# Four operands of a linear-attention kernel turned by block loads and 32x32 VectorE transposes

## The chip, the cores and the metric

The kernel runs on one core of one Trainium2 chip. The metric is the device time in microseconds, as the median of several runs. The core has five engines that each work through a queue of their own in order: TensorE (PE in the profile, its weight loads PEld), VectorE (DVE), ScalarE (ACT), GpSimd (POOL) and SyncE (SP, which here only issues DMAs). DMAs can be issued from SP's queue and from ScalarE's.

## What is computed

First a recurrence with a 40x40 state for each of 4 x 8 (batch, head) pairs over 768 tokens, then a mixture of four experts over 3072 tokens of width 320:

```
for t in range(S):
    y[:, :, t] = einsum('bhd,bhde->bhe', rt, state)
    Sa = einsum('bhde,bhe->bhd', state, at)
    state = state * wt[:, :, None, :] - einsum('bhd,bhe->bhde', Sa, bt) + einsum('bhd,bhe->bhde', vt, kt)
x = y with (batch, token) as rows and (head, channel) as 320 columns
p = domain_probs / (domain_probs.sum(-1) + 1e-9)
out = sum over e of p[:, e] * (relu(x @ w1[e]) @ w2[e])        # w1[e]: 320 x 1024
```

All of it is float32. Inputs r, k, v, w, a, b are stored as (batch, head, token, channel), so that a row of 40 channels, 160 bytes, is contiguous.

## The kernel before

**Units.** Tokens are taken in chunks of 64. A unit is one chunk of two batches, all eight heads: 24 units, in order of chunk. Its 128 partitions are 2 x 64 tokens ("token-major"), or, after a turn, 2 x 64 channels of a pair of heads of which 40 count ("channel-major"). Within a unit the recurrence is rewritten as matrix products between 64 tokens, with decays accumulated along the chunk, and a triangular solve in 32x32 blocks.

**Loads.** `load` brings each operand token-major, one DMA for each batch; V and R take three each, since their heads 4 to 7 are stored with neighbours swapped. All go through SP, 20 issues a unit (L188). Loads for unit u + 3 are issued in the loop's round u.

**`within(q)`** is the part of a unit that needs no state. It is a generator: each `yield` ends a piece, and the loop says which piece comes where. Its first piece turns W on TensorE (`turn`, L295: four transposes of 128x128 against the identity into one PSUM bank), copies it from PSUM on ScalarE one token to the right (L346) and takes the running product along tokens with a VectorE scan (L347): G, channel-major. `gl` is the product over the whole chunk. The second piece turns G back (pg) and forms gp = pg * W and a_tok = pg * A on VectorE, the reciprocal of gp (L365), and turns R and V. Then n_tok = -B / gp and k_tok = K / gp (L392, L395). Then A, N and K are turned and copied (`turned`, L369), and the score matrices are formed by `quadrants` (L327: 32 small matmuls, in 64x64 quarters of the array): `pc` from R and V, `pf` and `pe` from A, N, K; `pev` follows. `causal` is a masked copy on VectorE (L334).

**`substitute`** is the triangular solve: blocks of F are turned by VectorE into M (L445, L448), and a chain of some 66 operations follows on GpSimd, or on VectorE for units 0 and 1. `merge` turns the result Z back by two 32x32 transposes (Qc L495, QTc L497) and completes it with TensorE products pY, pQ; ScalarE copies it into QT (L527). **`step`** carries the state: prn (AT and state), psat, pxr, then pdy and the state's update. Its output Y goes to xT, channel-major, by small DMAs (L639), or by TensorE (L627) for the first units.

**The mixture** is cut into pieces that stand in a list `todo`: an `up` piece (24 matmuls, L654 and L662, then two ScalarE activations L667) or a `down` piece (L769, then adds on VectorE L680 and, after every second one, sums of hidden activations L763). w1 streams in pieces through SP (L238). `mix(n)` emits the next n pieces; `gap(0)` to `gap(3)` do this four times in each round of the loop, two pieces each in most rounds. So PE has mixture pieces between the recurrence's parts.

**Order.** The framework schedules what it is given; `keep_in_program_order` pins an instruction against the other pinned ones. PSUM has five banks for the recurrence ("big") and three for the mixture ("mm").

Of the kernel before, what the change touches and what calls it, by code (L numbers as in the profile page):

```python
# [15 lines left out]
def kernel(  # L16
# [12 lines left out]
):  # L29

# [98 lines left out]
    def kept(name, shape, n, value=0.0, eng=nc.gpsimd, lo=0):  # L129
# [15 lines left out]
    nat = {  # L145
        x: kept(f"nat{x}", of_64, n, float(x == "W"), nc.vector, D) for x, n in (("W", 2), ("R", 2), ("V", 2))
    }
    a_tok = kept("a_tok", of_64, 1, lo=D)
# [25 lines left out]
    def load(q, names):  # L174
        for x in names:
            if x in nat:
                t = nat[x]()
            else:
                t = sb.tile([P, H, D], FP32, name=f"nat{x}")
            q.n[x] = t  # L180
            for i, bb in enumerate(q.b):
                to, src = t[i * L:(i + 1) * L, :, 0:D], srcs[x][bb, :, q.c * L:(q.c + 1) * L, :]
                parts = ((slice(0, H), slice(0, H)),)
                if x in "VR":

                    parts = ((slice(0, 4), slice(0, 4)), (slice(5, H, 2), slice(4, H, 2)), (slice(4, H, 2), slice(5, H, 2)))
                for o, h in parts:
                    nc.sync.dma_start(out=to[:, o, :], in_=src[h].rearrange("h t e -> t h e"))  # L188
# [3 lines left out]
    for u, names in ((0, "W"), (1, "W"), (0, "ABKVR")):  # L192
        load(units[u], names)
# [111 lines left out]

    def head(j, s):
        return 2 * j + s

    def d_half(j, s):
        return s ^ (j // 2)  # L310

    def d_head(j, s):
        return 2 * j + d_half(j, s)

    BY_TOKENS = [(j, s, i) for j in range(NJ) for s, i in QUADS]
    BY_PAIRS = [(j + 2 * x, s, i) for i in range(2) for j in range(2) for s, x in QUADS]
# [16 lines left out]
    def causal(to, data):  # L333
        return nc.vector.copy_predicated(  # L334
            out=to, mask=mask_up[:, None, :].to_broadcast([P, data.shape[1], L]), data=data,
        )

    def within(q):

        n = q.n  # L340
        pw = by(turn("pw", tok(n["W"]))[:], L)
        q.G = G = sb.tile([P, 2 * NJ, L], FP32, name="G", tag="G", bufs=3)
        ins = nc.vector.memset(G[:, :, 0:1], 0.0)
        if q.u == 1:
            tc.keep_in_program_order(ins)
        nc.scalar.copy(out=G[:, :, 1:L], in_=pw[:, :, 0:L - 1])  # L346
        ins = nc.vector.tensor_tensor_scan(  # L347
            out=G[:].rearrange("p c i -> p (c i)"), data0=G[:].rearrange("p c i -> p (c i)"),
            data1=first[:].rearrange("p c i -> p (c i)"), initial=0.0, op0=ALU.mult, op1=ALU.add,
        )  # L350
        if q.u == 1:
            tc.keep_in_program_order(ins)
        q.gl = sb.tile([P, 2 * NJ, 1], FP32, name="gl", tag="gl", bufs=4)
        nc.scalar.copy(out=q.gl[:], in_=pw[:, :, L - 1:L])
        nc.vector.tensor_tensor(out=q.gl[:], in0=q.gl[:], in1=G[:, :, L - 1:L], op=ALU.mult)
        yield

        pg = by(turn("pg", tok(G), q.u == 2)[:], 64)[:, :, 0:D]
        gp = sb.tile([P, H, D], FP32, name="gp")
        ins = nc.vector.tensor_tensor(out=gp[:], in0=pg, in1=n["W"][:, :, 0:D], op=ALU.mult)  # L360
        if q.u == 1:
            tc.keep_in_program_order(ins)
        A = a_tok()
        nc.vector.tensor_tensor(out=A[:, :, 0:D], in0=pg, in1=n["A"][:], op=ALU.mult)
        nc.vector.reciprocal(out=gp[:], in_=gp[:])  # L365

        def turned(name, x, keep=False):
            t = sb.tile([P, NJ, P], FP32, name=name, tag=name if keep else "turned", bufs=2 if keep else 3)
            nc.scalar.copy(out=t[:].rearrange("p j t -> p (j t)"), in_=turn("p" + name, tok(x), q.u == 1)[:])  # L369
            return t  # L370

        def turn_rv():
            q.RT = turned("RT", n["R"], True)
            return turned("VT", n["V"])

        def causal_scores(VT):
            pc = quadrants(banks("pc"), 0, BY_TOKENS, L, lambda j, s, i: (
                d_half(j, s), i, j, of_pairs(VT, d_half(j, s), j, i), of_pairs(q.RT, d_half(j, s), j, i),
            ))
            for s in range(2):  # L380
                ins = causal(of_slot(q.VC[:], s)[:, :, D:D + L], pc[s])
                if q.start:
                    tc.keep_in_program_order(ins)

        if q.u == 1:
            yield
        if q.u > 0:
            VT = turn_rv()
            yield
# [5 lines left out]
        nc.vector.tensor_tensor(out=q.K[:, :, 0:D], in0=n["K"][:], in1=gp[:], op=ALU.mult)  # L395
        q.VC = VCs()
        if q.u > 0:
            nc.scalar.copy(out=q.VC[:, :, 0:D], in_=n["V"][:, :, 0:D])
        yield

        q.AT = turned("AT", A, True)
# [4 lines left out]
        if q.u > 0:  # L406
            causal_scores(VT)
# [4 lines left out]
            s, i ^ s, j, of_pairs(q.AT, s, j, i), of_pairs(NT, s, j, i),  # L412
        ))
        pe = quadrants(p, NJ * L, BY_TOKENS, L, lambda j, s, i: (
            s, i, j, of_pairs(KT, s, j, i), of_pairs(q.AT, s, j, i),
# [9 lines left out]
        if q.u == 0:  # L425
            tc.keep_in_program_order(nc.scalar.copy(out=q.VC[:, :, 0:D], in_=n["V"][:, :, 0:D]))
        q.EV = EVs()
        pev = quadrants(banks("pev"), 0, BY_TOKENS, D, lambda j, s, i: (
            i, i ^ s, j, ET[half(i), head(j, s), :], q.VC[half(i), d_head(j, s), 0:D],
# [571 lines left out]
```

## Time and profile before

| | us |
|---|---|
| median of 3 runs | 1162.93 (1161.68 to 1165.82) |
| profiled execution | 1161.04 |
| its span, first to last instruction | 1159.3 |
| PE busy | 1134.2 |
| DVE busy | 693.6 |
| ACT busy | 385.4 |
| POOL busy | 472.5 |
| DMA moved | 107.45 MB in 218853 packets |

The profile is one execution. Its page has the engines' busy times, the span in 40 slices, and groups of instructions by line, with busy time, the mean duration in ns, and the idle time ahead of them with what ended it. The chain of waits is followed back from the last instruction. Matmuls overlap in PE's pipeline, so their distance counts and not their duration.

### The profile page before, as it was taken

The numbers are of one execution on the slowest core, as the hardware profiler recorded it, in microseconds if no ns is written. First come the engines' busy times: TensorE is split into PE (matmuls) and PEld (weight loads), VectorE is DVE, ScalarE is ACT, GpSimd is POOL, SyncE is SP. The second block draws the span as 40 slices with busy tenths as digits, with TensorE's granted clock in tenths as the row PEclk, the third lists the DMA queues.
The fourth block names the chain that finished last, engine by engine and source line by source line (L and its number), as shares of the span: only waits on it lengthen the run. The fifth ranks groups of instructions, "written<-read, shape, count | busy, mean of one in ns | idle before, by whom it ended". The sixth has DMA issues, their size and how long they took to land.

```text
span 1159.3 us, 38763 instructions
## 1 busy us (share of the span) xinstructions
PE 1134.2 (98%) x16400; PEld 1014.2 (87%) x16400; DVE 693.6 (60%) x1466; ACT 385.4 (33%) x961; POOL 472.5 (41%) x1218
## 2 busy tenths in 40 slices
PE   7999999999999999999999999999999999999998
PEld 6887787798988999898989899998889898988887
DVE  7754556775665575666746655756567566543333
ACT  3332444334233333333342333333333423311110
POOL 4006555572462552643724625526336246240000
PEclk8899999999999999999999999999999999999999
DMA  4695433323333333243333333342333341221320
GB/s 68 196 278 109 106 76 85 88 67 92 94 93 94 86 89 98 65 112 71 93 93 85 100 96 78 91 96 73 101 75 93 91 105 49 76 88 52 104 91 12
DMA packets 218853, 107.45 MB, mean 93 GB/s; under 512 B 163720, under 2 KB 192056, under 8 KB 218680
## 3 DMA queue, kind: packets, MB, share of 16 engines
q1 hardware_dynamic: 218600, 104.93, 35.1%
q8 instruction: 130, 2.13, 0.7%
q14 instruction: 43, 0.35, 0.1%
q10 hardware_dynamic: 80, 0.04, 0.0%
HBM read 97.04 MB, written 3.93 MB: 87 GB/s over the span
## 4 chain that ended last, share of the span: by engine, by line
PE 92%; DMA 2%; ACT 2%; SPq 2%; issue 1%; DVE 1%; ACTq 0%; DVEq 0%
PE ph L662 30%; PE p L769 29%; PE ph L654 9%; PE pdy L327 3%; PE po L703 2%; PE psat L327 2%; PE pfe L327 2%; PE pxr L327 2%; SPq L188 2%; PE prn L327 2%; PE pc L327 1%; PE pQ L522 1%; PE pY L510 1%; PE pev L327 1%; DMA w<-in_moe_w_dram 1%; PE pg L295 1%
## 5 line engine op out<-in xcount | busy, mean ns | idle before, releaser
L662 PE MATMUL ph<-xT,w1p 128*128 128x256 f32 (+1 forms) x1520 | 343.6, 379 | 0.1
L471 POOL TENSOR_TENSOR Z<-M,Z 128x62 f32<-128x62 f32 (+7 forms) x352 | 164.8, 468 | 404.4 <-DVE M L464 378.5
L662 PEld LDWEIGHTS ph<-xT,w1p 128*128 128x128 f32 x1520 | 274.6, 191 | 62.3 <-issue 26.0
L484 POOL TENSOR_TENSOR Z<-Z 128x31 f32<-128x31 f32 (+7 forms) x704 | 247.3, 351 | 55.2
L763 DVE TENSOR_TENSOR a<-hs 128x512 f32<-128x512 f32 x220 | 153.5, 715 | 186.4 <-ACT hs L667 186.4
L667 ACT ACTIVATE hs<-ph 128x512 f32<-128x512 f32 (+1 forms) x208 | 117.2, 564 | 304.7 <-PE ph L662 304.2
L769 PE MATMUL p<-sums,a 128*128 128x160 f32 x1056 | 164.8, 299 | 0.0
L680 DVE SCALAR_TENSOR_TENSOR osb<-p,gate,osb 128x320 f32<-128x320 f32 (+1 forms) x243 | 108.4, 484 | 93.7 <-PE p L769 88.6
L769 PEld LDWEIGHTS p<-sums,a 128*128 128x128 f32 x1056 | 152.9, 190 | 2.2
L654 PE MATMUL ph<-xT,w1p 64*128 64x256 f32 (+1 forms) x760 | 109.6, 395 | 1.5 <-PE psat L327 1.0
L769 PE MATMUL p<-w,hs 128*128 128x160 f32 x704 | 102.9, 299 | 0.0
L769 PE MATMUL p<-w,a 128*128 128x160 f32 x704 | 102.8, 299 | 0.0
L769 PEld LDWEIGHTS p<-w,hs 128*128 128x128 f32 x704 | 100.2, 190 | 2.2
L769 PEld LDWEIGHTS p<-w,a 128*128 128x128 f32 x704 | 98.0, 190 | 0.0
L654 PEld LDWEIGHTS ph<-xT,w1p 64*128 64x128 f32 x760 | 67.2, 186 | 13.7 <-issue 3.3
L503 POOL COPY QT<-QTc 32x256 f32<-32x256 f32 x96 | 38.8, 404 | 97.1 <-DVE QTc L497 87.3
L448 DVE STREAM_TRANSPOSE M<-blocks 128x1024 f32<-128x1024 f32 x24 | 47.0, 1957 | 33.1 <-ACT blocks L445 32.4
L365 DVE RECIPROCAL gp<-gp 128x320 f32<-128x320 f32 x24 | 51.3, 2137 | 0.0
L527 ACT COPY QT<-pQ 32x256 f32<-32x256 f32 x48 | 17.4, 362 | 83.3 <-PE pQ L522 82.8
L369 ACT COPY RT<-pRT 128x512 f32<-128x512 f32 x24 | 14.1, 586 | 93.1 <-PE pRT L295 93.0
L595 ACT COPY RS<-pxr 64x256 f32<-64x256 f32 x88 | 32.3, 367 | 34.9 <-issue 25.9
L327 PE MATMUL pdy<-VC,k_tok 64*64 64x104 f32 (+1 forms) x768 | 38.8, 261 | 0.0
(143 smaller groups left out, 1423.5 us busy)
## 6 DMA issues: line engine op xcount, KB each, us to landing
w1p<-in_moe_w_dram SPq DMA_DIRECT2D x95, 512.0 KB
w1p<-in_moe_w_dram SPq DMA_DIRECT2D x190, 64.0 KB
w<-in_moe_w_dram SPq DMA_DIRECT2D x4, 1280.0 KB
sums<-in_moe_w_dram SPq DMA_DIRECT2D x9, 512.0 KB
natW<-in_w_dram SPq DMA_DIRECT2D x48, 80.0 KB
natA<-in_a_dram SPq DMA_DIRECT2D x48, 80.0 KB
natB<-in_b_dram SPq DMA_DIRECT2D x48, 80.0 KB
natK<-in_k_dram SPq DMA_DIRECT2D x48, 80.0 KB
```

The costliest lines, as they stand in the source:

```text
L327: nc.tensor.matmul(out=p[row][half(col), lo + at * out_cols:lo + (at + 1) * out_cols], lhsT=lhsT, rhs=rhs, start=(n == 0), stop=(n == len( ...
L365: nc.vector.reciprocal(out=gp[:], in_=gp[:])
L448: ins = nc.vector.transpose(out=M[:], in_=cols)
L471: ins = eng.tensor_tensor(out=Z[:, 1:3, 0:n, j + 1:Q], in0=M[:, j:j + 2, None, j + 1:Q].to_broadcast([P, 2, n, m]), in1=Z[:, here, 0:n, j: ...
L484: eng.tensor_tensor(out=z[:, 0], in0=z[:, 0], in1=z[:, x], op=ALU.add)
L503: ins = nc.gpsimd.tensor_copy(out=q.QT[quarter(i), :, quarter(i % 2)], in_=QTc[quarter(i)])
L654: nc.tensor.matmul(out=ph[i][:, f, :], lhsT=w1.last[i * DT:(i + 1) * DT, f, :], rhs=xT[i * DT:(i + 1) * DT, 2, :], start=(f == 0), stop=False,
L662: nc.tensor.matmul(out=ph[i][:, f, :], lhsT=w1.main[:, g, at * P:(at + 1) * P], rhs=xT[:, g, :], start=False, stop=(g == 1 and f == HF // ...
L667: nc.scalar.activation(out=h[:, i * HF // 2:(i + 1) * HF // 2, 0:n], in_=ph[i][:], func=ACTF.Relu,)
L680: nc.vector.scalar_tensor_tensor(out=to, in0=p, scalar=sc, in1=to, op0=ALU.mult, op1=ALU.add)
L763: nc.vector.tensor_tensor(out=t[:], in0=x, in1=y, op=op)
L769: nc.tensor.matmul(out=p[:, n * HD:(n + 1) * HD], lhsT=a[:, f, :], rhs=b[:, f, :], start=(f == 0), stop=(f == HF - 1),)
```

## The change

W, A, R and V are no longer turned on TensorE. `load_raw` brings each of them in blocks. The 16 heads of a unit are taken in pairs, and partitions are pairs of neighbouring tokens. A block has 32 token pairs on 32 partitions and, for each head, 72 or 48 contiguous values: channels 0 to 31 of both tokens (with what lies between), or channels 32 to 39. Four such blocks fill 128 partitions: W and A take 4 DMAs each, R and V 8 each, since every second head of theirs goes to the other half ("d swapped by odd pairs"). Each has one buffer. `turn_raw` then transposes 32x32 squares on VectorE, 128x512 in one instruction, with the two tokens of a pair written side by side; W takes two of 128x256. The scan's input, VT, RT and AT come from that directly, channel-major. A's product with its decay is taken channel-major (AT * G, 128x512), after the turn, where it was taken token-major from PSUM (pg * A, 128x320) before. `gl` is a small VectorE copy. W, B, K and V are also loaded token-major, one DMA for each batch; A and R are not.

V's and R's heads go to the halves by `s ^ (j % 2)` where it was `s ^ (j // 2)`; the token-major V is no longer swapped, and the orders of the quadrant products and the masked copies follow. The turns of V and R stand in the third piece of `within`, after k_tok, and A's too.

In the loop SP issues W's and A's blocks (8) and the natural loads (8) of unit u + 3. V's and R's 16 blocks go into a list `later`, from which ScalarE issues three after each mixture piece (six where a gap has one piece), pinned; what is left goes ahead of the next unit's third piece. At the start, ScalarE issues unit 0's A and V blocks and SP the rest, and 20 warm-up matmuls stand where there were 6 and 4.

```diff
@@ -142,10 +146,8 @@
     srcs = {"W": w, "A": a, "B": b, "K": k, "V": v, "R": r}
     of_64 = [P, H, 64]
-    nat = {
-        x: kept(f"nat{x}", of_64, n, float(x == "W"), nc.vector, D) for x, n in (("W", 2), ("R", 2), ("V", 2))
-    }
-    a_tok = kept("a_tok", of_64, 1, lo=D)
+    raw = {x: kept(f"raw{x}", [P, 2 * NJ, 2 * D], 1, 0.0, nc.vector, D + D - Q) for x in "WARV"}
     k_tok, n_tok = (kept(x, of_64, 2, lo=D) for x in ("k_tok", "n_tok"))
     both = [P, H, D + L]
@@ -173,24 +175,51 @@
     def load(q, names):
         for x in names:
-            if x in nat:
-                t = nat[x]()
-            else:
-                t = sb.tile([P, H, D], FP32, name=f"nat{x}")
-            q.n[x] = t
+            q.n[x] = t = sb.tile([P, H, D], FP32, name=f"nat{x}", tag=f"nat{x}", bufs=2 if x in "WV" else 1)
             for i, bb in enumerate(q.b):
-                to, src = t[i * L:(i + 1) * L, :, 0:D], srcs[x][bb, :, q.c * L:(q.c + 1) * L, :]
-                parts = ((slice(0, H), slice(0, H)),)
-                if x in "VR":
-                    parts = ((slice(0, 4), slice(0, 4)), (slice(5, H, 2), slice(4, H, 2)), (slice(4, H, 2), slice(5, H, 2)))
-                for o, h in parts:
-                    nc.sync.dma_start(out=to[:, o, :], in_=src[h].rearrange("h t e -> t h e"))
+                nc.sync.dma_start(
+                    out=t[i * L:(i + 1) * L], in_=srcs[x][bb, :, q.c * L:(q.c + 1) * L, :].rearrange("h t e -> t h e"),
+                )
+    def load_raw(q, names):
+        moves = []
+        for x in names:
+            q.n["raw" + x] = t = raw[x]()
+            heads = srcs[x].rearrange("b h t e -> (b h) t e")[q.b[0] * H:(q.b[1] + 1) * H, q.c * L:(q.c + 1) * L, :]
+            heads = heads.rearrange("n (x two) e -> x n (two e)", two=2)
+            for r in range(2):
+                if x in "RV":
+                    sets = ((slice(0, 8, 2), slice(r, 16, 4)), (slice(1, 8, 2), slice(3 - r, 16, 4)))
+                else:
+                    sets = ((slice(0, 8), slice(r, 16, 2)),)
+                for n, hs in sets:
+                    for y, w_ in enumerate((D + Q, 2 * D - Q)):
+                        o = slice(64 * r + Q * y, 64 * r + Q * y + Q)
+                        moves.append(lambda eng, out=t[o, n, 0:w_], in_=heads[:, hs, Q * y:Q * y + w_]: eng.dma_start(out=out, in_=in_))
+        return moves
+    def go(moves, eng=None):
+        for move in moves:
+            move(eng or nc.sync)
+    def turn_raw(out, t):
+        return nc.vector.transpose(
+            out=out.rearrange("p n (x two) -> p n two x", two=2),
+            in_=t.rearrange("p n (two e) -> p n two e", two=2)[:, :, :, 0:Q],
+        )
     for u in range(3):
         begin(u)
-    for u, names in ((0, "W"), (1, "W"), (0, "ABKVR")):
-        load(units[u], names)
+    go(load_raw(units[0], "W"))
+    load(units[0], "WBK")
+    go(load_raw(units[0], "A"), nc.scalar)
+    load(units[0], "V")
+    go(load_raw(units[0], "V"), nc.scalar)
+    go(load_raw(units[0], "R"))
@@ -303,17 +332,21 @@
     def of_pairs(x, hf, j, i):
         return x[half(hf), j, part(i)]
+    def of_slots(x, hf, j, i, n=64):
+        return x[64 * hf:64 * hf + n, 4 * i + j, :]
     def head(j, s):
         return 2 * j + s
     def d_half(j, s):
-        return s ^ (j // 2)
-    def d_head(j, s):
-        return 2 * j + d_half(j, s)
+        return s ^ (j % 2)
+    def of_d_half(x, r):
+        return x.rearrange("p (jj four) e -> p jj four e", four=4)[:, :, slice(1, 3) if r else slice(0, 4, 3), :]
...
     def within(q):
         n = q.n
-        pw = by(turn("pw", tok(n["W"]))[:], L)
-        q.G = G = sb.tile([P, 2 * NJ, L], FP32, name="G", tag="G", bufs=3)
-        ins = nc.vector.memset(G[:, :, 0:1], 0.0)
-        if q.u == 1:
-            tc.keep_in_program_order(ins)
-        nc.scalar.copy(out=G[:, :, 1:L], in_=pw[:, :, 0:L - 1])
-        ins = nc.vector.tensor_tensor_scan(
-            out=G[:].rearrange("p c i -> p (c i)"), data0=G[:].rearrange("p c i -> p (c i)"),
+        def pin(ins, also=False):
+            if q.u == 1 or also:
+                tc.keep_in_program_order(ins)
+        G = sb.tile([P, 2 * NJ * L + 1], FP32, name="G", tag="G", bufs=3)
+        q.G = Gv = G[:, 0:2 * NJ * L].rearrange("p (c t) -> p c t", t=L)
+        ahead = G[:, 1:2 * NJ * L + 1].rearrange("p (j i t) -> p i j t", i=2, t=L)
+        for i in range(2):
+            pin(turn_raw(ahead[:, i], n["rawW"][:, NJ * i:NJ * i + NJ, :]))
+        q.gl = sb.tile([P, 2 * NJ, 1], FP32, name="gl", tag="gl", bufs=4)
+        pin(nc.vector.tensor_copy(out=q.gl[:, :, 0], in_=G[:, L::L]))
+        pin(nc.vector.memset(Gv[:, :, 0:1], 0.0))
+        pin(nc.vector.tensor_tensor_scan(
+            out=G[:, 0:2 * NJ * L], data0=G[:, 0:2 * NJ * L],
             data1=first[:].rearrange("p c i -> p (c i)"), initial=0.0, op0=ALU.mult, op1=ALU.add,
-        )
-        if q.u == 1:
-            tc.keep_in_program_order(ins)
-        q.gl = sb.tile([P, 2 * NJ, 1], FP32, name="gl", tag="gl", bufs=4)
-        nc.scalar.copy(out=q.gl[:], in_=pw[:, :, L - 1:L])
-        nc.vector.tensor_tensor(out=q.gl[:], in0=q.gl[:], in1=G[:, :, L - 1:L], op=ALU.mult)
-        yield
-        pg = by(turn("pg", tok(G), q.u == 2)[:], 64)[:, :, 0:D]
+        ))
+        nc.vector.tensor_tensor(out=q.gl[:], in0=q.gl[:], in1=Gv[:, :, L - 1:L], op=ALU.mult)
+        yield
+        pg = by(turn("pg", tok(Gv), q.u == 2)[:], 64)[:, :, 0:D]
         gp = sb.tile([P, H, D], FP32, name="gp")
-        ins = nc.vector.tensor_tensor(out=gp[:], in0=pg, in1=n["W"][:, :, 0:D], op=ALU.mult)
-        if q.u == 1:
-            tc.keep_in_program_order(ins)
-        A = a_tok()
-        nc.vector.tensor_tensor(out=A[:, :, 0:D], in0=pg, in1=n["A"][:], op=ALU.mult)
+        pin(nc.vector.tensor_tensor(out=gp[:], in0=pg, in1=n["W"][:], op=ALU.mult))
         nc.vector.reciprocal(out=gp[:], in_=gp[:])
-        def turned(name, x, keep=False):
-            t = sb.tile([P, NJ, P], FP32, name=name, tag=name if keep else "turned", bufs=2 if keep else 3)
+        yield
+        def turned(name, x):
+            t = sb.tile([P, NJ, P], FP32, name=name, tag="turned", bufs=3)
             nc.scalar.copy(out=t[:].rearrange("p j t -> p (j t)"), in_=turn("p" + name, tok(x), q.u == 1)[:])
             return t
-        def turn_rv():
-            q.RT = turned("RT", n["R"], True)
-            return turned("VT", n["V"])
-        def causal_scores(VT):
+        def causal_scores():
             pc = quadrants(banks("pc"), 0, BY_TOKENS, L, lambda j, s, i: (
-                d_half(j, s), i, j, of_pairs(VT, d_half(j, s), j, i), of_pairs(q.RT, d_half(j, s), j, i),
+                d_half(j, s), i, j, of_slots(VT, d_half(j, s), j, i, D), of_slots(q.RT, d_half(j, s), j, i, D),
             ))
-            for s in range(2):
-                ins = causal(of_slot(q.VC[:], s)[:, :, D:D + L], pc[s])
-                if q.start:
-                    tc.keep_in_program_order(ins)
-        if q.u == 1:
-            yield
-        if q.u > 0:
-            VT = turn_rv()
-            yield
+            for r in range(2):
+                pin(causal(of_d_half(q.VC[:, :, D:D + L], r), pc[r]), q.start)
         q.K, q.N = k_tok(), n_tok()
         nc.vector.scalar_tensor_tensor(
             out=q.N[:, :, 0:D], in0=n["B"][:], scalar=-1.0, in1=gp[:], op0=ALU.mult, op1=ALU.mult,
         )
         nc.vector.tensor_tensor(out=q.K[:, :, 0:D], in0=n["K"][:], in1=gp[:], op=ALU.mult)
+        q.AT = sb.tile([P, 2 * NJ, L], FP32, name="AT", tag="AT", bufs=2)
+        turn_raw(q.AT[:], n["rawA"][:])
+        at_ij = q.AT[:].rearrange("p (i j) t -> p i j t", i=2)
+        nc.vector.tensor_tensor(out=at_ij, in0=at_ij, in1=Gv.rearrange("p (j i) t -> p i j t", i=2), op=ALU.mult)
         q.VC = VCs()
         if q.u > 0:
-            nc.scalar.copy(out=q.VC[:, :, 0:D], in_=n["V"][:, :, 0:D])
-        yield
-        q.AT = turned("AT", A, True)
+            nc.scalar.copy(out=q.VC[:, :, 0:D], in_=n["V"][:])
+        VT = sb.tile([P, 2 * NJ, L], FP32, name="VT", tag="turned", bufs=3)
+        q.RT = sb.tile([P, 2 * NJ, L], FP32, name="RT", tag="RT", bufs=2)
+        turn_raw(VT[:], n["rawV"][:])
+        turn_raw(q.RT[:], n["rawR"][:])
+        yield
         NT = turned("NT", q.N)
         KT = turned("KT", q.K)
         yield
         if q.u > 0:
-            causal_scores(VT)
+            causal_scores()
             yield
...
@@ -571,29 +602,26 @@
...
         yield
         p = banks("pxr")
         px = quadrants(p, 0, BY_TOKENS, L, lambda j, s, i: (
-            d_half(j, s), i, j, SaT[half(d_half(j, s)), j, i ^ s, :], of_pairs(q.RT, d_half(j, s), j, i),
+            d_half(j, s), i, j, SaT[half(d_half(j, s)), j, i ^ s, :], of_slots(q.RT, d_half(j, s), j, i),
         ))
         if not q.start:
             prs = quadrants(p, NJ * L, BY_PAIRS, L, lambda j, s, i: (
-                d_half(j, s), s, 2 * (j % 2) + i, SN[half(d_half(j, s)), s, 2 * i + j % 2, :],
-                of_pairs(q.RT, d_half(j, s), j, i),
+                d_half(j, s), s, 2 * (j // 2) + i, SN[half(d_half(j, s)), s, 2 * i + j // 2, :],
+                of_slots(q.RT, d_half(j, s), j, i),
             ))
         for x in range(2):
...
@@ -825,12 +853,19 @@
             before = [lambda e=e: down_1(e), lambda e=e, second=second: second(e)]
         last[:] = before
-    todo, last = [], []
+    todo, last, later = [], [], []
+    def begin_later(n):
+        for move in later[:n]:
+            tc.keep_in_program_order(move(nc.scalar))
+        del later[:n]
     def mix(n):
         for piece in todo[:n]:
             piece()
+            begin_later(3 if n > 1 else 6)
         del todo[:n]
     def run(gen, n=99):
@@ -856,11 +891,13 @@
             tc.keep_in_program_order(ins)
     ws = [within(units[u]) for u in range(3)]
-    keep_warm(6)
+    keep_warm(20)
     run(ws[0], 1)
-    keep_warm(4)
+    go(load_raw(units[1], "W"))
     run(ws[0], 1)
-    load(units[1], "ABKVR")
+    load(units[1], "WBKV")
+    run(ws[0], 1)
+    go(load_raw(units[1], "AVR"))
     load_probs()
     run(ws[1], 1)
     run(ws[0], 2)
@@ -870,15 +907,16 @@
     m, s = merge(units[0]), begin_step(0)
     run(m, 1)
     run(ws[0])
-    load(units[2], "WVR")
+    go(load_raw(units[2], "W"))
+    load(units[2], "WBKV")
     for e in range(2):
         load_piece()
         load_piece()
         load_w2(e)
     run(ws[1], 1)
     keep_warm(36)
-    run(ws[1], 2)
-    load(units[2], "ABK")
+    run(ws[1], 1)
+    go(load_raw(units[2], "AVR"))
     load_piece()
     run(m)
     run(s, 4)
@@ -900,7 +938,8 @@
     run(ws[2], 2)
     run(s, 2)
     run(ws[2], 1)
-    load(begin(3), srcs)
+    load(begin(3), "WBKV")
+    go(load_raw(units[3], "WAVR"))
     substitute(units[2], nc.gpsimd)
     mix(1)
     w_next = ws[2]
@@ -938,13 +977,16 @@
             mixture_of_unit(q)
         elif q.bp:
             mixture_of_chunk(units[u - 1:u + 1], chunks_x[q.c])
+        begin_later(len(later))
         run(w, 1)
         if not early:
             run(m, 1)
         gap(1)
         if u + 3 < NU:
-            load(begin(u + 3), srcs)
+            go(load_raw(begin(u + 3), "WA"))
+            load(units[u + 3], "WBKV")
+            later.extend(load_raw(units[u + 3], "VR"))
         run(w, 2)
         if not early:
             run(s_next, 1)
```

## Prediction

> **What bounds the kernel now.** I read the page first, its engine table and its 40 slices.
>
> ```profile
> span 1159.3 us, 38763 instructions
> PE 1134.2 (98%) x16400; PEld 1014.2 (87%) x16400; DVE 693.6 (60%) x1466; ACT 385.4 (33%) x961; POOL 472.5 (41%) x1218
> PEclk8899999999999999999999999999999999999999
> DMA  4695433323333333243333333342333341221320
> ```
>
> TensorE is busy for 98% of the span and its granted clock is full after the second slice; DMA is heavy only in slices two and three. A busy PE may hide waits, so I next read the chain of waits, in order of time, around one unit in the middle:
>
> ```profile
> 601.34 0.44 PE pw L295 x4
> 601.77 0.60 PE pev L327 x32
> ...
> 612.39 0.44 PE pg L295 x4
> 612.83 0.44 PE pRT L295 x4
> 613.27 0.44 PE pVT L295 x4
> 613.70 1.74 PE pdy L327 x61
> ...
> 623.42 0.44 PE pAT L295 x4
> 623.85 0.44 PE pNT L295 x4
> 624.29 0.44 PE pKT L295 x4
> 624.73 0.62 PE pc L327 x32
> ```
>
> Nothing but PE is on it, and pw returns 45.36 us later: that is one unit. Each group of four transposes takes 0.44 us of PE's queue (not the 0.27 us that one matmul is shown to last, since they overlap). The windows view over exactly one unit says how much room the others have:
>
> ```profile
> 600.00:645.36 45.36, 45.36 (x686) 41.18 (x686) 28.19 (x59) 16.02 (x40) 20.25 (x51) 1.00 0.32 86
> ```
>
> The columns are PE, PEld, DVE, ACT, POOL, then clock, DMA share and GB/s: PE 45.36 of 45.36, VectorE 28.19, ScalarE 16.02.
>
> **The change, part by part.** *TensorE.* pw, pRT, pVT and pAT go; pg, pNT and pKT stay. 4 x 0.44 = 1.76 us a unit, all on the path. Units 2 to 23 have theirs where PE carries the path: 22 x 1.76 = 38.7 us. Units 0 and 1 belong to the start, below. The quadrant products keep their number and sizes; only their order changes (nothing).
>
> *VectorE.* It gains three 128x512 turns (A, V, R), two of 128x256 (W), one 128x512 product and a small copy, and loses a_tok. The trace has these rows (busy us, mean ns):
>
> ```profile
> L495 DVE STREAM_TRANSPOSE Qc<-Z 128x256 f32<-128x256 f32 x24 | 15.1, 628 | 36.6 <-POOL Z L484 36.6
> L497 DVE STREAM_TRANSPOSE QTc<-Qc 128x256 f32<-128x256 f32 x24 | 10.7, 445 | 0.6
> L461 DVE TENSOR_TENSOR Z<-M 128x512 f32<-128x512 f32 x24 | 16.6, 691 | 0.7
> ```
>
> A 128x512 turn lies between 0.69 us (any 512-column operation) and 1.26 (twice Qc, whose writes are scattered). I take twice QTc, 0.89, for it reads whole runs of 32 as the new turns do; their writes step by only two elements. W's halves are 0.45 each. Sum: 3 x 0.89 + 2 x 0.45 + 0.70 + 0.17 (gl, as L355) - 0.48 (a_tok) = 4.0 us; VectorE goes from 28.2 of 45.4 to 32.2 of 43.6, 74%. Average room is not enough, so I follow the tight stretch. At 610.26 VectorE begins the adds of a down piece and runs without a gap to the end of k_tok at 619.99, now 0.40 sooner without a_tok: 619.6. Then come A's turn, its product, V's and R's turn, 3 x 0.89 + 0.70 = 3.4: 623.0. PE wants them at pc, which moves from 624.73 up by three turns (1.32) to 623.4: 0.4 us to spare. Qc and QTc (1.08) follow, done at 624.05 for pY at 626.28 - 1.32 = 624.96. So I put the cost at nothing, but the cover is thin: at 0.69 a turn it is 1.0 us, at 1.26 pc is 0.7 us late. W's turns fall in a 3.5 us hole of VectorE before the sums of hs at 608.7, and cost nothing; were that hole shut, the 1.2 us would meet PE's next down piece.
> The Trainium skill, page "VectorE: DVE Perf Modes", section "Rules for kernel authors", speaks against this: for a whole 128x128 transpose it prefers TensorE where PSUM will do. By it each tensor pays 0.45 us more (0.89 against 0.44), a loss where VectorE were the bound; the unit above shows that PE is.
>
> *ScalarE and the loads.* ScalarE loses the copies of pw (0.58 + 0.17), RT, VT and AT (0.59 each): 2.5 us. It gains 16 DMA issues a unit, V's and R's blocks, six per gap. The issues of natV on SP last 0.595/0.606/1.514 us (min/median/max). Sixteen at 0.62 are 9.9 us, so ScalarE goes to 23.4 of 43.6. What counts is who is queued behind them. Six stand after the activation that ends at 632.26; the next there is QT's copy, which waits for pQ (ends 636.59) and which psat needs at 637.68:
>
> ```profile
> 631.66 0.60 ACT L667 ACTIVATE hs<-ph 128x512 f32<-128x512 f32 x1 [1.07 <-PE ph L662]
> 636.64 0.75 ACT L527 COPY QT<-pQ 32x256 f32<-32x256 f32 x2 [4.38 <-PE pQ L522]
> ```
>
> 6 x 0.62 = 3.7 us in a hole of 4.4: nothing, so long as an issue stays under 0.72 us. The one issue of before that ScalarE makes (the last store) took 0.56 us while SP was issuing too.
> SP has 16 issues a unit (8 raw W and A, 8 natural) where it had 20: 2.5 us less. Its raw A must wait for VectorE's turn of the unit before, as each raw tile has one buffer; behind it stand B, K, V, the xT moves and w1p. SP runs ahead of PE there: it waits 263 us in all (L238, for PE ph) until a w1p buffer is free. Packets: a unit had 6 x 1024 of 160 bytes; now 4 x 1024 of these and 4 x 1024 of 288 or 192. 2048 more at the queue's mean (35.1% x 16 x 1159.3 / 218600 = 30 ns) are 3.8 us of the sixteen engines: share 0.32 to 0.42, hidden. V's and R's last four issues follow the activation that ends at 608.7, so they end by 611.2 and land by 613.2 (1.97 us, as natR at the start); V's turn comes at 621.2.
>
> For short stalls that this working misses I allow 0.1 us a unit, an estimate: 20 units, 2 us.
>
> *The start.* This is where the change costs. The chain opens with 21 issues of SP, 0.65 us apart, then natR's landing:
>
> ```profile
> 14.95 1.97 DMA natR<-in_r_dram
> 16.91 0.40 ACT blocks L445
> 17.33 0.47 ACT VC L426
> ```
>
> Unit 1's first scan is pinned on VectorE ahead of unit 0's M (17.64 before). Its W now comes raw, behind 20 issues of unit 0: the 24th ends at 0.8 + 24 x 0.655 = 16.5, lands near 18.5; two turns, copy, memset, scan and gl (2.6), ET (0.8) and blocks (0.6) put M at 22.5, 4.9 late. If it is put ahead of R's loads, under 1 us is left. Unit 1's own turns add 3.4 - 0.5 = 2.9 us of VectorE where k_tok ends at 37.8 and the next product is due at 39.56: 1.2 late. RT, VT and AT leave the chain there (0.45 + 0.44 + 0.59): -1.5. Then SP has 20 issues of unit 2 in place of 6 while DMA is saturated by the weights (hidden), and 32 of unit 3 in place of 20, where the chain runs over SP from 90.55 to 98.09 and natR to 100.9: 12 x 0.61 = 7.3 later, of which some 4 is given back since R is wanted a piece later: 3.3. Sum 4.9 + 1.2 - 1.5 + 3.3 = 7.9, between 0 and 15. The ten extra warm-up matmuls run while PE would wait for W (nothing; 10 x 0.13 if not).
>
> *Sum.* 1159.3 - 38.7 + 2 + 7.9 = 1130.5 span; 1.7 outside it (the profiled execution took 1161.04) gives 1132.2; the median of before is 1.9 above that execution: 1134.
>
> **Rivals.**
> *All hidden, start too.* Nothing but TensorE's turns and those of units 0 and 1: 1162.9 - 38.7 - 1.5 = 1123. For it: pins and scheduling may put unit 1's W early. Against: one buffer each and 12 to 14 more issues twice.
> *VectorE's third piece becomes late.* At 1.26 us a turn or over, or with slower products beside POOL, pc and pY wait about 1 us in each of 22 units: 1134 + 22 = 1156. For it: ten us of VectorE without a gap before pc. Against: QTc's 445 ns.
> *ScalarE's issues stand before QT's copy (slower).* If SP and ScalarE take turns, an issue lasts 2 x 0.606 = 1.21 us; six are 7.3 where the hole is 4.4, so psat is 2.9 us late in each of the 20 units that have such issues: 1134 + 58 = 1192. It decides from (4.4 + 1.76) / 6 = 1.03 us an issue, when the unit's gain is gone. For it: SP's issues reach 1.5 to 1.9 us beside heavy traffic, and SP is busy through 628 to 640. Against: the 0.56 us at the end.
> The page "Perfetto Trace Analysis", section "DMA Instruction — HWDGE (DVE, Sync)", has the issuing sequencers lock one descriptor generator in turn; that would make this rival's case, and no steady stretch of this trace shows two queues issuing.
> *The change doesn't do what it says*: turns wait for blocks that land late, as the single raw buffers refill only after use; then VectorE, not PE, paces early units: within the second rival's price.
>
> **How the numbers follow.** Forecast 0.55 (1123 to 1148, the start between 0 and 15 and stalls up to 0.5 us a unit), all hidden 0.12, third piece late 0.17 (some of it within no change), ScalarE 0.16. The range takes in the first three and the cheap end of the last (0.85 us an issue, 1134 + 20 x 0.7 = 1148, to 0.95, 1134 + 26 = 1160): 1118 to 1165. A measurement of this kernel tells 0.3%, 3.5 us, from no change. Faster 0.80, same 0.03, slower 0.17.
>
> **What would show it.** Right: a unit of 43.6 us, PE at 100% in it, L295 down from 28 matmuls to 12, VectorE near 32 us, ScalarE's issues 0.6 us each and M of unit 0 starting at 18 to 23. Wrong: PE idle or waiting at pc for VT or RT, psat for QT's copy, or ScalarE issues over 0.75 us; a unit above 44.5; or a start that is over 15 us longer.

## The result, and where the profile says the time went

The changed kernel takes 1229.97 us (median of 4 runs, 1226.71 to 1233.65) against 1162.35 us for the kernel before (4 runs, 1161.68 to 1165.82): ratio 1.0576, 95% interval 1.054 to 1.0613. The forecast was 1134 us. The profiled execution took 1226.71 us. Its page, the lines that answer to the first four of before:

```profile
span 1225.0 us, 38138 instructions
PE 1135.7 (93%) x16036; PEld 1002.9 (82%) x16036; DVE 757.2 (62%) x1560; ACT 335.6 (27%) x841; POOL 471.9 (39%) x1217
PEclk7979999989999999999999899998899999999999
DMA  6687465534344343443442443433335423222320
```

TensorE executes 364 matmuls fewer and is busy for as long as before, 1135.7 us, in a longer span: it lost share (98% to 93%) and clock, for the row PEclk now has eights in the middle of the run. The chain of waits in order of time, where unit 14's pQ ends, shows both losses:

```profile
672.08 1.06 PE ph L682 x8
673.14 3.65 PE ph L690 x16
...
681.14 0.62 PE pQ L553 x32
681.76 1.09 PE pfe L360 x64
682.85 3.76 issue
686.61 2.36 PE psat L360 x59
688.97 2.01 PE ph L682 x8
690.98 4.80 PE ph L690 x16
```

Where there was no pause, TensorE now stands still for 3.76 us ahead of psat; after it, the 24 matmuls of ph take 2.01 + 4.80 = 6.81 us, where the same number took 1.06 + 3.65 = 4.71 some seventeen microseconds earlier. The windows view (columns: stretch, length, PE, PEld, DVE, ACT, POOL busy, clock, DMA share, GB/s) gives the granted clock of a stretch without a pause and of the one with it, then of the whole steady part, unit 4's pQ to unit 22's; the last line is the steady part of the kernel before:

```profile
650.00:680.00 30.00, 30.00 (x357) 27.06 (x356) 22.41 (x46) 8.88 (x21) 18.02 (x44) 1.00 0.32 77
680.00:700.00 20.00, 16.24 (x285) 14.01 (x287) 8.12 (x16) 5.05 (x14) 3.92 (x13) 0.83 0.45 111
203.60:1065.70 862.10, 810.86 (x11874) 721.71 (x11874) 559.19 (x1127) 250.54 (x627) 374.43 (x954) 0.96 0.40 97
187.00:1000.20 813.20, 807.65 (x12170) 729.38 (x12172) 516.22 (x1061) 287.19 (x717) 378.98 (x954) 1.00 0.34 88
```

Why psat waits stands in ScalarE's timeline. QT's copy, whose output psat reads, is behind six moves of V; the bracket names what released it:

```profile
676.78 1.08 ACT L695 ACTIVATE hs<-ph 128x512 f32<-128x512 f32 x2
678.59 7.51 ACTq L201 DMA_DIRECT2D rawV<-in_v_dram  x6
686.15 0.75 ACT L558 COPY QT<-pQ 32x256 f32<-32x256 f32 x2 [8.29 <-DMA rawV<-in_v_dram]
```

pQ had ended at 681.76. The six moves hold ScalarE's queue for 7.5 us, but not by issuing: over the run a move issues in 0.44 us (median), 0.47 (mean). They wait. By the trace's semaphore events the transfers of SyncE and ScalarE end on the same eight completion semaphores, taken in turn in program order, and a move starts only when the transfer that had its semaphore before it has landed. Followed back one by one, ScalarE's moves waited 113 us in all, 73.3 of it (43 times) for a w1p piece that SyncE had issued, 16.0 for rawW, 11.3 for natK, 8.1 for natB. A move of V needs nothing of w1p. In the list of waits of the steady part (us in total, times, longest), what ScalarE's copies wait for is therefore a transfer that neither of them reads:

```profile
ACT QT L558 <- DMA rawV<-in_v_dram: 77.8, 11, 9.0
ACT EV L464 <- DMA rawR<-in_r_dram: 37.6, 9, 4.7
```

Adding up, over these 18 units, the time from the first start of each tile's matmuls to the first start of the next tile's gives the account of the steady part (us; the last three columns are runs told below):

| | before | after | e1 | e5 | e11 |
|---|---|---|---|---|---|
| pw, pRT, pVT, pAT | 34.9 | 0 | 0 | 0 | 0 |
| pfe (and the pause behind it) | 16.8 | 59.8 | 16.8 | 18.6 | 16.8 |
| psat | 22.8 | 36.6 | 24.6 | 135.0 (with filler) | 24.9 |
| ph | 332.6 | 355.1 | 338.1 | 332.9 | 337.4 |
| all else | 406.0 | 410.6 | 410.3 | 410.1 | 409.2 |
| sum | 813.1 | 862.1 | 789.8 | 896.6 | 788.3 |

So -34.9 from the turns, +56.8 from pfe and psat, +22.5 from ph, +4.6 elsewhere: +49.0. Each of the two losses is part pause, part lower clock. Adding up TensorE's gaps of over 0.15 us in the trace, 39.6 of the 56.8 are pauses and 17.2 are matmuls that run slower; of ph's 22.5, 5.8 are pauses inside ph and 16.7 slower matmuls. The windows agree: TensorE is idle for 51.2 us of the steady part (862.10 - 810.86) where it was 5.6, and a clock of 0.96 over 862 us costs some 34 us. QT's copy starts 3.1 us after pQ's end on average in units 6 to 21, where it was 0.05. The start, up to unit 4's pQ, grew from 187.0 to 203.6 us (+16.6), the tail by 0.2.

### The profile page after: what moved, and what is told of

The parts are those of the page before. It is cut to its first block, busy times and chain, and to the rows that moved or that the text cites. A ratio compares the mean times of both kernels' runs of the same rounds, so it can differ in the third digit from the quotient of the medians.

```text
span 1225.0 us, 38138 instructions
## 1 busy us (share of the span) xinstructions
PE 1135.7 (93%) x16036; PEld 1002.9 (82%) x16036; DVE 757.2 (62%) x1560; ACT 335.6 (27%) x841; POOL 471.9 (39%) x1217
## 4 chain that ended last, share of the span: by engine, by line
PE 85%; DVE 6%; issue 4%; DMA 3%; ACT 1%; SPq 1%; ACTq 0%; DVEq 0%
PE ph L690 28%; PE p L797 26%; PE ph L682 9%; PE pdy L360 3%; PE psat L360 3%; PE pfe L360 2%; PE pxr L360 2%; PE prn L360 2%; PE po L731 1%; PE pc L360 1%; PE pQ L553 1%; PE pY L541 1%; DMA rawV<-in_v_dram 1%; PE pNT L324 1%; PE pev L360 1%
## 5 line engine op out<-in xcount | busy, mean ns | idle before, releaser
L690 PE MATMUL ph<-xT,w1p 128*128 128x256 f32 (+1 forms) x1520 | 352.8, 386 | 0.0
L690 PEld LDWEIGHTS ph<-xT,w1p 128*128 128x128 f32 x1520 | 280.5, 195 | 66.8 <-issue 27.0
L502 POOL TENSOR_TENSOR Z<-M,Z 128x62 f32<-128x62 f32 (+7 forms) x352 | 151.8, 431 | 457.7 <-DVE M L495 431.9
L682 PE MATMUL ph<-xT,w1p 64*128 64x256 f32 (+1 forms) x760 | 119.9, 429 | 5.1 <-issue 4.1
L534 POOL COPY QT<-QTc 32x256 f32<-32x256 f32 x96 | 53.1, 553 | 109.8 <-DVE QTc L528 99.3
L682 PEld LDWEIGHTS ph<-xT,w1p 64*128 64x128 f32 x760 | 72.9, 205 | 20.3 <-issue 6.8
L360 PE MATMUL psat<-QT,RH 64*64 64x64 f32 x704 | 25.8, 261 | 42.3 <-issue 40.1
L360 PEld LDWEIGHTS psat<-QT,RH 64*64 64x64 f32 x704 | 20.8, 164 | 47.7 <-issue 46.6
L371 DVE COPY_PREDICATED ET<-mask_up,pfe 128x256 f32<-128x256 int32 x48 | 18.6, 439 | 62.0 <-ACT F L450 61.9
```

Source lines behind the costliest of these rows:

```text
L360: nc.tensor.matmul(out=p[row][half(col), lo + at * out_cols:lo + (at + 1) * out_cols], lhsT=lhsT, rhs=rhs, start=(n == 0), stop=(n == len( ...
L502: ins = eng.tensor_tensor(out=Z[:, 1:3, 0:n, j + 1:Q], in0=M[:, j:j + 2, None, j + 1:Q].to_broadcast([P, 2, n, m]), in1=Z[:, here, 0:n, j: ...
L534: ins = nc.gpsimd.tensor_copy(out=q.QT[quarter(i), :, quarter(i % 2)], in_=QTc[quarter(i)])
L682: nc.tensor.matmul(out=ph[i][:, f, :], lhsT=w1.last[i * DT:(i + 1) * DT, f, :], rhs=xT[i * DT:(i + 1) * DT, 2, :], start=(f == 0), stop=False,
L690: nc.tensor.matmul(out=ph[i][:, f, :], lhsT=w1.main[:, g, at * P:(at + 1) * P], rhs=xT[:, g, :], start=False, stop=(g == 1 and f == HF // ...
```

## Experiments

**The moves out of ScalarE's queue (e1).** In `begin_later`:

```diff
-            tc.keep_in_program_order(move(nc.scalar))
+            tc.keep_in_program_order(move(nc.sync))
```

> The changed kernel with one word changed in begin_later: the moves of V and R for later units are issued from SyncE's queue, as all others are, and no longer from ScalarE's; the layout, the VectorE turns and the number of moves stay. Theory (a move in ScalarE's queue waits until a SyncE transfer that had its completion semaphore has landed, QT's copy stands behind it, psat behind that, and the granted clock falls after each pause of TensorE): the copy of QT follows pQ at once again, the 57 us between pfe and the end of psat and the 22 us of ph go, the time is 1140 to 1160 and the unit's pitch about 43.6 us. Rival (the turns on VectorE, the 128-byte pieces of the moves or the traffic they make are the cost): the time stays at 1215 or more.

1164.68 us, ratio to before 1.0003 (0.9975 to 1.003). QT's copy follows pQ in every unit from 6 on,

```profile
646.37 0.75 ACT L558 COPY QT<-pQ 32x256 f32<-32x256 f32 x2 [3.78 <-PE pQ L553]
```

a unit without a stall is 43.6 us, and the steady part is 23.3 us shorter than before. Turns on VectorE, layout, bytes and pieces (of 288 and 192 bytes, not the 128 that the expectation says) are those of the changed kernel, so none of them is its cost in the steady part; the rival falls. The time is a little above the range, since the start got worse still: 210.5 us, with SyncE now issuing everything.

**ScalarE's queue, but not in front of QT's copy (e2).**

```diff
-            begin_later(3 if n > 1 else 6)
+            if moves:                      # False in the gap ahead of pQ
+                begin_later(4 if n > 1 else 8)
```

> The changed kernel with ScalarE still issuing every move of V and R, but none of them in the gap before pQ and QT's copy: those six move to the gaps behind psat and behind the second attention matmul. Theory (place: it hurts because QT's copy is queued behind the moves): 1150 to 1175, with the waits for moves still in ScalarE's queue but ahead of work that is not urgent. Rival (that ScalarE issues at all, or the traffic of the moves): about 1230, as the changed kernel.

1164.72 us, ratio 1.0004 (0.9976 to 1.0031), steady part 795.8, start 204.6. ScalarE issues as many moves as in the changed kernel and they still wait, some 64 us over the run in place of 113 (eight of V hold its queue for 6.4 us at 652.4), now ahead of EV's copy, which has slack. It is the place that costs; what the issuing and the waits cost in the new places is at most the 6 us by which this steady part is longer than e1's.

**One part alone, in the kernel before (e3).** V's and R's natural loads go into the same list; in the loop:

```diff
-            load(begin(u + 3), srcs)
+            load(begin(u + 3), "WABK")
+            load(units[u + 3], "VR", later)
```

> The kernel before, its layout and TensorE transposes untouched, with one part of the change: V's and R's loads of units 4 and on (12 moves a unit) are issued from ScalarE's queue, in the same three gaps. Theory (issuing them there makes QT's copy late): 1210 to 1245, the copy of QT late by 3 us or more in most units. Rival (the blocks and the VectorE turns are the cost, not the queue): about 1162.

1217.61 us, ratio 1.0444 (1.0389 to 1.0498), without a single block or VectorE turn. The same picture in ScalarE's timeline, though QT's copy is late by 1.5 us on average in units 6 to 21, half of what was expected:

```profile
485.79 6.93 ACTq L189 DMA_DIRECT2D natV<-in_v_dram  x6
492.76 0.75 ACT L532 COPY QT<-pQ 32x256 f32<-32x256 f32 x2 [6.54 <-DMA natV<-in_v_dram]
```

Most of the loss is reproduced by the queue alone: 37.6 us in the steady part (psat's wait and the clock again: pfe 34.6, ph 345.7) and 17.8 in the start, where moves of units 4 and 5 already stand in ScalarE's queue.

**Issuing or waiting (e10).** The changed kernel with only the weights' queue changed, so that ScalarE's moves no longer share semaphores with them:

```diff
-            tc.keep_in_program_order(nc.sync.dma_start(out=to, in_=src))
+            eng = nc.gpsimd if k >= 20 else nc.sync
+            tc.keep_in_program_order(eng.dma_start(out=to, in_=src))
```

> The changed kernel with V's and R's moves left in ScalarE's queue in front of QT's copy, but the expert weights from the 21st piece on issued from GpSimdE, whose transfers end on completion semaphores of their own. Theory (a ScalarE move waits for the SyncE transfer that had its semaphore before, most often a slow weight piece: 73 us of the 112 such waits): QT's copy is late by about 1 us a unit in place of 3, ScalarE's waits for w1p are gone, and the part of the time that they cost with it, 15 to 35 us, unless GpSimdE, which now waits for the weights' buffers, holds up the substitution. Rival (the moves are slow in ScalarE's queue for what it holds itself, or the bytes ahead of them): QT's copy stays late by 3 us a unit.

The six moves now take 2.74 us in front of QT's copy, 0.46 each, and the copy starts as pQ ends (650.98):

```profile
646.05 2.74 ACTq L201 DMA_DIRECT2D rawV<-in_v_dram  x6
651.02 0.75 ACT L559 COPY QT<-pQ 32x256 f32<-32x256 f32 x2 [4.38 <-DMA rawV<-in_v_dram]
```

(The bracket names the last semaphore by the profile; the copy was held by pQ.) ScalarE's waits for w1p fell from 73.3 us to 1.6. So six issues do fit into the hole, as the prediction had it; what it left out was the wait. I had expected a delay of 1 us to stay, and from unit 7 on there is none (0.05 us). The slower pace of this kernel doesn't make the room: from the moves' start to pQ's end it is 4.9 us here and 3.2 in the changed kernel at 678.59, and 2.74 fits into either. Its traffic is thinner, though, 87 GB/s on average in place of 101, and this run can't part that from the semaphores; what names w1p's is the count of waits above. The kernel itself is far slower, 1417.74 us, ratio 1.2161 (1.2078 to 1.2244): GpSimdE comes to the weights only after its substitution, and TensorE waits for them, in 600 us of the run

```profile
PE ph L683 <- DMA w1p<-in_moe_w_dram: 119.2, 10, 12.8
```

**The clock (e5).** Filler ahead of psat, in psat's own bank, units 4 to 22:

```diff
+        for _ in range(28 if 4 <= q.u < 23 else 0):
+            tc.keep_in_program_order(
+                nc.tensor.matmul(out=p[0][:, 0:P], lhsT=ident[:], rhs=ident[:], start=True, stop=True))
```

> The changed kernel with 28 added matmuls on TensorE in the pause between pfe and psat, units 4 to 22 (they write psat's own bank before psat does, about 3.1 us of work, and their result is not used). Theory (ph is 22 us longer in the steady part because the granted clock falls after TensorE's pause): ph is back at the time it has in the kernel before, the clock is 0.98 or more, and the time falls to 1200 to 1215 although work is added. Rival (ph is longer for another reason, such as the traffic): 1230 or more, ph unchanged.

1271.14 us, ratio 1.0902 (1.0834 to 1.0969): the time missed, for the filler is twice too long, 6.45 us for 28 in the chain. What it was made for came out: TensorE no longer pauses ahead of psat, the clock of the steady part is 1.00 (0.96 in the changed kernel), and ph is back at 332.9 us.

```profile
652.93 1.09 PE pfe L360 x64
654.02 6.45 PE psat L591 x56
660.47 1.07 PE psat L360 x64
661.54 1.06 PE ph L686 x8
662.61 3.65 PE ph L694 x16
```

ScalarE's moves and all their bytes are still there and QT's copy is still 2.9 us late on average, so it was TensorE's pauses that brought the lower clock. Not all of ph's +22.5 us is the clock: the unit is longer here (50.1 us), and the short pauses inside ph go too. The 16.7 us above are the clock's share of ph; with the 17.2 in pfe and psat it comes to 34 us. The Trainium skill, page "TensorE: Matmul & The Clock Gate", section "HAM oscillation — how this bites in real kernels", tells of the same pattern, a wait in each tile that ends the full clock, and draws it for waits of 3 to 5 us. Here shorter ones do it too. Of the 14 pauses between pfe and psat, the eleven of 1.6 to 5.6 us each brought 3.4 or 6.8 us at a granted clock of 0.50 (the pause of 1.68 us at 346.07, for one: the window 348.50:351.90 has 0.50); the three of 0.9 to 1.4 us brought none, and neither did one of 2.3 us inside psat.

**The start: only issues (e7), and the first units' moves in another queue (e6).** e7 adds 36 small moves to the kernel before, e6 changes e2:

```diff
+            tc.keep_in_program_order(nc.sync.dma_start(out=small[n:n + 1, :], in_=r[0, 0, n:n + 1, :]))
...
-    go(load_raw(units[1], "AVR"))
+    go(load_raw(units[1], "AVR"), nc.gpsimd)
-    go(load_raw(units[2], "AVR"))
+    go(load_raw(units[2], "AVR"), nc.gpsimd)
-    go(load_raw(units[3], "WAVR"))
+    go(load_raw(units[3], "WAVR"), nc.gpsimd)
```

> The kernel before with 36 added moves of 160 bytes each in SyncE's queue, 12 behind the loads of each of units 1, 2 and 3: the issues of the changed kernel's start without their bytes or their pieces (what they fetch is not used). Theory Q (number of issues in the queue): about 36 x 0.5 us more in SyncE's queue ahead of the weights, start 8 to 18 us longer, the time 1170 to 1182. Theory D (pieces on the DMA engines): at most 3 us longer, 1160 to 1166.

> The version e2_none_before_qt with the block moves of A, V and R of units 1 and 2 and of W, A, V and R of unit 3 (64 moves) issued from GpSimdE's queue in place of SyncE's: the same bytes in the same pieces, but SyncE comes to the expert weights some 30 us of issuing earlier over the start. Theory Q (the start is bound by the order and number of issues in SyncE's queue): pQ of unit 4 at 185 to 195, the time 1143 to 1155. Theory D (by the time the small pieces take on the DMA engines, or by their arrival): pQ of unit 4 stays at 200 or later, the time 1158 or more.

Why these: SyncE's timeline, first of before, then of the changed kernel, between the first weights and the fourth block of down weights (w):

```profile
52.64 2.22 SPq L188 DMA_DIRECT2D natA<-in_a_dram  x2
54.96 3.74 SPq L188 DMA_DIRECT2D natB<-in_b_dram  x2
58.80 2.59 SPq L188 DMA_DIRECT2D natK<-in_k_dram  x2
61.43 3.59 SPq L238 DMA_DIRECT2D w1p<-in_moe_w_dram  x6
...
72.76 0.59 SPq L255 DMA_DIRECT2D w<-in_moe_w_dram  x1
```

```profile
60.13 3.96 SPq L201 DMA_DIRECT2D rawA<-in_a_dram  x4
64.21 6.88 SPq L201 DMA_DIRECT2D rawV<-in_v_dram  x8
71.19 4.88 SPq L201 DMA_DIRECT2D rawR<-in_r_dram  x8
76.11 3.38 SPq L267 DMA_DIRECT2D w1p<-in_moe_w_dram  x6
...
87.75 0.59 SPq L284 DMA_DIRECT2D w<-in_moe_w_dram  x1
```

The weights are issued 15 us later, and not because the DMA engines are full. Between 69 and 78 us, while SyncE issues V and R, they are busy for two to five tenths and move 40 to 113 GB/s. The changed kernel's DMA view, 40 to 130 us in 40 slices of 2.25 us:

```profile
DMA  0265889999999324586899999998567743356001
GB/s 0 44 97 96 260 237 249 352 334 295 310 305 147 51 40 67 113 254 209 283 299 366 321 285 332 368 286 174 99 95 126 127 82 62 63 87 228 0 0 30
```

e7: 1165.01 us, ratio 0.9997 (0.9978 to 1.0016); unit 4's pQ at 191.4, 4.4 us later than before. Its time is in D's range, its start between the two: issues alone, which wait for nothing, explain a quarter of the 16.6 us. e6: 1154.74 us, ratio 0.9894 (0.9844 to 0.9944), pQ of unit 4 at 193.4 in place of e2's 204.6, with the same bytes. So most of the start, 11.2 of the 17.6 us by which e2's is longer than before, goes with the moves in SyncE's queue, by their issues and their waits together. One reserve stays: the page counts only 2176 packets for the 64 moves in GpSimdE's queue, and 9088 fewer in all, so some of the gain may be cheaper packets; no run parts the two. In e6, units 4 and 5 still stumble over ScalarE's queue, now with SaT's copy behind it (with that queue freed too, in e11 below, unit 4's pQ comes another 7.1 us earlier):

```profile
240.99 7.61 ACTq L201 DMA_DIRECT2D rawV<-in_v_dram  x8
248.64 0.37 ACT L600 COPY SaT<-psat 128x256 f32<-128x256 f32 x1 [7.06 <-DMA rawV<-in_v_dram]
```

**First units by natural loads (e8), inconclusive.** e2 with units 0 to 3 turned on TensorE again:

```diff
-    go(load_raw(units[2], "AVR"))
+    load(units[2], "ABK")
...
+        if q.u < 4:
+            nc.scalar.copy(out=G[:, 1:2 * NJ * L + 1], in_=turn("pw", tok(n["W"]))[:])
```

> The version with no move in front of QT's copy (e2_none_before_qt), and units 0 to 3 as they were before the change: W, A, R and V of these four come by natural loads (12 moves a unit in place of 32) and TensorE turns them; from unit 4 on blocks and VectorE turns. Theory (the start is 17 us longer because the first units' many small moves stand in SyncE's queue and on the DMA engines ahead of the expert weights): unit 4's pQ is back at 185 to 192 us, the steady part stays near 796 us, the time is 1140 to 1152, under both kernels. Rival (the start is longer for what VectorE and ScalarE do there, or because unit 4's first blocks are late whatever stands before them): pQ of unit 4 at 200 or more, the time about 1160.

1163.03 us, ratio 0.9973 (0.9939 to 1.0007); pQ of unit 4 at 202.4. These are the rival's numbers, but they don't show its causes. Units 0 to 3 compute other values here than the reference's, so only the schedule is read. For want of room each of the four tensors has one buffer where the kernel before has two for W, R and V, and unit 0's pQ is already 9.4 us later than before. More than one thing was changed, and the run tells nothing about which.

**Both repairs (e11), and everything in GpSimdE's queue (e12).** e11 is e6 with e1's `move(nc.sync)`, in all three gaps, e12 the same with `move(nc.gpsimd)`.

> The changed kernel with ScalarE's queue free of V's and R's moves (SyncE issues them from unit 4 on, as in e1_moves_on_sp) and the first units' 64 block moves in GpSimdE's queue (as in e6_start_gpsimd). Theory (the change's gain of TensorE time is there and was hidden by two queues: ScalarE's in the steady part, SyncE's in the start): unit 4's pQ near 193 us as in e6, the stretch from there to unit 22's pQ 787 to 795 us as in e1, the time 1138 to 1148, under both kernels. Rival (the two repairs are worth the same microseconds, or SyncE's moves come too late once the start is shorter): 1152 or more.

1132.95 us (1130.69 to 1135.94), ratio 0.9751 (0.9725 to 0.9777): faster than both kernels, and than the range expected. Unit 4's pQ is at 186.3, a unit without a stall 43.6 us, the steady part 788.3.

```profile
PE 1098.2 (97%) x16036; PEld 978.1 (86%) x16036; DVE 757.2 (67%) x1560; ACT 331.8 (29%) x841; POOL 506.6 (45%) x1281
PEclk7889999999999999999999999999999999999999
```

> As e11_gpsimd_then_sp, with the steady part's 16 moves of V and R a unit issued from GpSimdE's queue too, in the three gaps. A move costs GpSimdE 0.55 to 0.62 us there in the start of e6, so some 9 us a unit, beside a substitution that keeps it busy for some 20 us of the 43.6. Theory (it has the room): 1138 to 1150. Rival (a move that waits in GpSimdE's queue for a turn of VectorE holds the substitution up, as the weights did in e10): 1165 or more, QT's row of unit u + 2 late.

1394.78 us, ratio 1.1991 (1.1952 to 1.2029). The room on average was there, but not the place. The rival's time came by the reverse of its mechanism: the moves don't hold the substitution up, they stand behind it. GpSimdE's substitution runs until 519.79, and only then come the last two moves of V:

```profile
519.28 0.51 POOL L515 TENSOR_TENSOR Z<-Z 128x8 f32<-128x8 f32 x2
519.79 1.11 POOL L201 DMA_DIRECT2D rawV<-in_v_dram  x2
```

VectorE's turn of V is next in VectorE's order and waits for them, the adds of osb behind it free PE's banks late, and PE pauses for 9.9 us in ph, once a unit:

```profile
DVE VT L210 <- DMA rawV<-in_v_dram: 174.4, 10, 17.7
```

## Where the prediction was right and where it failed

*TensorE.* Right. 1.76 us a unit was said; the four groups cost 1.94 before (34.9 / 18) and are gone, and e1's, e2's and e11's unit is the 43.6 us of the forecast.

*VectorE.* Right, and on the safe side of its range: a 128x512 turn takes 0.70 us (0.89 was taken, 0.69 to 1.26 the range), a 128x256 turn of W 0.41 (0.45).

```profile
L210 DVE STREAM_TRANSPOSE G<-rawW x48: 391/406/1812, 6.0 to 1008.0; 128x256 f32<-128x256 f32 x48
L210 DVE STREAM_TRANSPOSE AT<-rawA x24: 654/701/1486, 7.2 to 1012.4; 128x512 f32<-128x512 f32 x24
```

VectorE is busy for 31.1 us a unit (559.19 / 18; 32.2 was said) and pc costs the same 9.4 us over 18 units as before, in e1 and e11 too, at the unit of 43.6 us. The cover of 0.4 us at pc held.

*ScalarE.* The step that failed: "6 x 0.62 = 3.7 us in a hole of 4.4: nothing, so long as an issue stays under 0.72 us". An issue is 0.47 us, well under, so six are 2.8 us (the hole is 3.8 us in e1), and the hole was overrun all the same. The step counted how long each move takes to issue and not how long each waits, though just beside it the same working had listed the waits of SyncE's queue. A move in ScalarE's queue is also an instruction with a wait, and behind it stood the copy that psat needs: +56.8 us in pfe and psat over 18 units. e1, e2 and e10 show it from three sides.

*The rival on that place* (0.16, 1192 us) had the place, the victim and nearly the price: QT's copy 2.9 us late in a unit was said, 3.1 measured. Its mechanism was wrong: issues did not last 1.21 us through taking turns (0.47 on ScalarE, where 7 of 333 lasted longer than 1.21; SyncE's issues 0.59 after, 0.61 before). Its trace test, "psat for QT's copy", is what the trace shows.

*The clock* was in no term. The rival's 58 us became 79 in pfe, psat and ph: 45 of pauses, and 34 of the lower clock that followed them.

*The start.* Its first term held: unit 0's M starts at 21.05 (22.5 said, 17.64 before). The mis-sized term is "20 issues of unit 2 in place of 6 while DMA is saturated by the weights (hidden)": the weights stand behind those issues, and come 15 us later. By the forecast's terms unit 4's pQ should have come 0.9 us later than before: 7.9, less 4 x 1.76 for the turns of units 2 to 5, which lie ahead of it. It came 16.6 later. e11, which has the same blocks and turns there, has it 0.7 us earlier than before.

*e11 beside the forecast.* With both queues freed the rest of the sum holds: the start is 1.6 us better than its terms (-0.7 against +0.9), the steady part 5.1 worse (-24.8 against -31.7 + 1.8). Units 13 and 20 are 4 us longer than the rest; behind unit 13's pQ the chain shows a pause of 2.7 us inside psat, whose cause I haven't found (the kernel before has two in the same place, of 1.0 and 1.3 us), and it costs more than itself, for ph then takes 6.35 us:

```profile
576.09 2.68 issue
578.77 0.33 PE psat L360 x5
579.10 1.63 PE ph L682 x8
580.73 4.72 PE ph L690 x16
```

## What to carry to other kernels

In these runs, moving DMA issues to a compute engine's queue put every wait of these DMAs in front of that engine's next instruction, the wait for a completion semaphore that another queue's slow transfer still holds among them; the length of an issue said nothing about that. Ask for each such move what it must wait for and what small copy stands behind it, and put moves behind the urgent copy or in a queue that feeds nobody. Price a pause of TensorE with the clock that follows it.

## What was not expected of the hardware

The Trainium skill, page "DMA: Bandwidth & Descriptors", section "Issuing engines are not separate DMA queues", says that issuing from several engines saves only the sequencer's time. These runs show that it can also cost: 54 us in e3 with no other edit. Eight semaphores shared by two queues tie a 24 KB move to a 512 KB weight piece.

A pause of 3.76 us on TensorE was followed by 24 matmuls at 1.45 times their time (6.81 against 4.71), and one of 2.68 us by 1.35 times; over the 18 units the lower clock cost some 34 us beside 45 us of pauses.

GpSimdE's queue issued a block move in 0.55 us (median, 0.77 at most) in the start of e6, where it had little else that was urgent; there it did better for them than SyncE's, and in e12's steady part it was the worst of the three.
